# Turned z of the last channel block: one transfer per eight rows, 128-row products, and a new order of the queues

## The chip, the cores and the metric

The kernel runs on one core of a Trainium2 chip. The core has a matrix engine (TensorE, PE in the profile, with its weight loads as PEld), VectorE (DVE), ScalarE (ACT), GpSimd (POOL) and SyncE (SP). SP and POOL are used here mostly to issue transfers: SP feeds queue q1 of the profile's table of queues, POOL feeds q0, and both are served by the same 16 DMA engines. The metric is the device time of one execution in microseconds, the median of several runs; lower is better.

## The reference

An S4 convolution block and an MLP block with adaptive layer normalisation, over one sequence of 2048 positions with 512 channels (D) and 1792 hidden units (F), all in float32. Cut to what matters:

```python
def _A_ref(u, A_re, A_im, B_re, B_im, C_re, C_im, log_dt, Dskip):
    dt = exp(log_dt)[:, None]
    P = exp((dt * (A_re + 1j*A_im))[:, :, None] * arange(L))
    K = einsum("dn,dnl,dn->dl", Cc, P, dt * Bc).real          # a kernel of 2048 taps per channel
    Yf = rfft(pad(u)) * rfft(pad(K))                          # long convolution by FFT
    return irfft(Yf)[:L] + u * Dskip

mod = (silu(c) @ w_mod).reshape(6, D)                         # sa, ca, ga, sb, cb, gb
h = layernorm(x) * (1 + ca) + sa
x = x + ga * _A_ref(h, ...)
h = layernorm(x) * (1 + cb) + sb
x = x + gb * (mish(h @ w1 + b1) @ w2)
```

## The kernel before

**Tiling.** The 512 channels are four blocks of 128 (b = 0 to 3). The Fourier transforms are done as matrix products in two stages, with 64 frequency columns times 32 rows. A block goes through eight steps v = 8b .. 8b+7 (s = v mod 8). In step v, `s_ubu`/`s_ug` and `s_ubk` make the two transforms of the eight rows s, `s_prod` multiplies them on DVE, `s_t1` transposes the result on PE, ACT copies it to the tile `yt`, and `s_invb` (L606) does the first inverse stage on PE (the bank `pib`) with the constants `mi`, copies it on ACT to the tile `z` and writes `z` on SP to DRAM, to `zd[b]`. The tile `z` has three buffers: the copy of step v waits until the write of step v-3 has landed.

**Turning.** The second inverse stage needs the data turned: rows on the partitions. So `zd[b]`, 64 rows of 64 columns times 128 channels, is read back into `zt` tiles. In blocks 0 to 2 that is `s_zl` (L621) and `zt_load` (L615), eight transfers of 64 rows for a whole block once all of its z is written; for the last block it is `zt_rows` (L961) within `drain`, two sets of eight rows at a time in four transfers (one for each group of 16 columns, j, which goes to 32 partitions of its own), and the last two sets singly. `inva_mm` and, for the last block, `inva_half` (L968) are the products of the second inverse stage, into the banks `pia`; `inva_half` contracts 32 partitions into 32 rows for each of 16 places. `inva_add` (L667) adds the residual x on DVE and writes the result to DRAM (`x2d`), on the queue named in `bulk[0]`.

**The drain.** `drain` (L940) is the code between the main loop and the MLP, and where this change mostly sits. Its eight steps v = 24..31 finish the last block, while the weights `w1` are loaded (`w1_load`, POOL, tiles `w1s` with three buffers) and split into high and low parts (`w1_split`, ACT and DVE), and block 2's `zt` is read. Behind the steps come the products of blocks 2 and 3, the bias rows of the MLP (`bias_rows`, `bias_sum`: products of `w1` with a row of the modulation), the layer normalisation of the first quarter of the rows (`ln_stats`, `ln_scales` with `rsqrt`, `ln_qs`), its transposition (`ln_tq`, banks `pln`) and `ln_h`, which makes the left operand `hh` of the MLP. The gate of the MLP, gb, is made early by `gate_row` (L480), written to DRAM as one row and read back to all partitions (`gbb`) in the drain. The last block is called b in `drain`, the third b-1.

**Order.** Instructions of DVE, ACT and PE within the drain are held in the order of the code (`InOrder`), those of DVE and ACT up to the second step f of the MLP; what stands outside this, among it the transfers of SP and POOL, a scheduler orders by priority. Each queue takes its transfers in order: a transfer that waits for a semaphore holds up what stands behind it on that queue.

**The MLP.** Behind the drain, 14 steps f handle the first quarter of the rows with plain products (`mm1_plain`, `mm2`), and `load_w2` (L1049) loads each `w2` piece on SP, multiplies it with `gbb` on DVE, splits it and stores it for the three later quarters.

## Time and profile before

| | us |
|---|---|
| median of 3 runs | 721.03 (718.92 to 723.68) |
| the profiled execution | 722.1 |
| its span, first to last instruction | 720.3 |
| from the drain's first step to the MLP's first product | about 341 to 403 |
| from the MLP's first product to the end | 403.1 to 720.3 |

PE is busy for 641.7 us of the span (89%), DVE for 496.4 (69%), ACT for 373.5 (52%) and POOL for 88.5 (12%). The mean granted PE clock is 0.964 of full speed. The queues moved 116.07 MB, 82.18 MB of it on q1 (SP) and 32.91 MB on q0 (POOL).

Nearly all rows of this profile have line L127, since a helper records every instruction of PE, DVE and ACT; such rows are told apart by their tiles. Transfers have the line of their call. In a timeline a row gives start and length in us, engine, line, operation, out<-in with the shape, the count of instructions merged into it, and in brackets how long the engine had been idle before it and what ended that. A float32 product is recorded as two MATMULs, so that 16 products are x32.

### The profile page before, as it was taken

To read this page: it belongs to the slowest core of one execution; us is meant where nothing else is said; L and a number is where in the kernel's file an instruction comes from. 1 tells how busy PE (TensorE), PEld (TensorE's weight loads), DVE (VectorE), ACT (ScalarE), POOL (GpSimd) and SP (SyncE) were. 2 spreads that over 40 slices of the span, in tenths; PEclk is the share of its full clock that TensorE was granted. 3 is DMA by queue.
4 is the path that set the end of the run, shared out by engine and by line. 5 is a ranking of instruction groups with operands and counts; after the bars stand their busy time and mean duration, and the time that the engine had idled before them with its cause. 6 is when DMAs were issued, how large, how long until landed. Compare 5 with 4: busy or idle time off the path is not lost.

```text
span 720.3 us, 15347 instructions
## 1 busy us (share of the span) xinstructions
PE 641.7 (89%) x6163; PEld 519.9 (72%) x6192; DVE 496.4 (69%) x1008; ACT 373.5 (52%) x620; POOL 88.5 (12%) x178
## 2 busy tenths in 40 slices
PE   0587686999999999999967999989999999999996
PEld 0353354777778877888841788878988898998995
DVE  6999976889899969994843799448336733563332
ACT  3665478556967686664630654443346244443231
POOL 1000530060106200001401000000100010010100
PEclk9969899999999999999978999989999999999999
DMA  9929788674229743565996498627432653264222
GB/s 235 228 110 294 169 193 199 186 178 119 63 72 213 184 118 99 132 180 140 268 216 152 144 325 285 211 71 204 135 117 89 199 163 107 89 190 133 87 88 59
DMA packets 108761, 116.07 MB, mean 161 GB/s; under 512 B 13009, under 2 KB 84945, under 8 KB 108050
## 3 DMA queue, kind: packets, MB, share of 16 engines
q1 hardware_dynamic: 94034, 82.18, 41.7%
q0 software_dynamic: 14656, 32.91, 16.3%
q8 instruction: 49, 0.80, 0.5%
q14 instruction: 22, 0.18, 0.1%
HBM read 80.44 MB, written 32.51 MB: 157 GB/s over the span
## 4 chain that ended last, share of the span: by engine, by line
PE 74%; DVE 10%; DMA 7%; ACT 5%; issue 3%; SPq 1%; DVEq 0%; ACTq 0%
PE pr L127 30%; PE pp L127 10%; PE pub L127 6%; PE pang L127 6%; PE pkb L127 4%; PE pkg L127 4%; PE pib L127 4%; PE pka L127 3%; DVE ec L127 2%; DMA zd<-z 2%; DVE raw L127 2%; PE pt L127 2%; ACT ec L127 2%; PE pbias L127 1%; DMA cT<-in_c 1%
## 5 line engine op out<-in xcount | busy, mean ns | idle before, releaser
L127 DVE TENSOR_TENSOR ec<-ec,m 128x1024 f32<-128x1024 f32 (+1 forms) x96 | 97.4, 1043 | 13.4 <-ACT ec L127 13.1
L127 ACT ACTIVATE ec<-pang 128x1024 f32<-128x1024 f32 x64 | 65.1, 1034 | 53.2 <-PE pang L127 53.2
L127 PE MATMUL pr<-hh,w 128*128 128x256 f32 (+1 forms) x420 | 77.9, 327 | 1.2 <-DVE hh L127 1.2
L127 PEld LDWEIGHTS pr<-hh,w 128*128 128x128 f32 x420 | 67.4, 189 | 12.7 <-DVE hh L127 1.5
L127 DVE TENSOR_TENSOR mh<-x,pr 128x256 f32<-128x256 f32 x63 | 26.4, 420 | 68.4 <-PE pr L127 68.2
L127 PE MATMUL pp<-w,mah 128*128 128x512 f32 x224 | 71.0, 398 | 0.8 <-DVE xf L127 0.8
L127 PE MATMUL pr<-w,mah 128*128 128x512 f32 x224 | 70.4, 396 | 0.0
L127 ACT ACTIVATE mh<-pr,b 128x256 f32<-128x256 f32 (+1 forms) x35 | 19.6, 560 | 80.7 <-PE pr L127 80.7
L127 DVE TENSOR_TENSOR m<-co 128x1024 f32<-128x1024 f32 (+1 forms) x64 | 59.7, 953 | 2.5 <-ACT co L127 2.2
L127 ACT ACTIVATE mh<-mh,b 128x256 f32<-128x256 f32 x63 | 32.1, 510 | 51.4 <-DVE mh L127 51.2
L127 DVE TENSOR_TENSOR mal<-mh,mah 128x512 fp32r<-128x512 f32 x56 | 38.5, 688 | 25.4 <-ACT mah L127 25.4
L1052 POOL DMA_DIRECT2D w<-w2d x42 | 22.2, 529 | 264.5 <-PE pp L127 249.4
L127 PE MATMUL pp<-w,mal 128*128 128x512 f32 x112 | 44.1, 394 | 0.0
L127 PE MATMUL pr<-w,mal 128*128 128x512 f32 x112 | 44.1, 394 | 0.0
L127 PEld LDWEIGHTS pp<-w,mah 128*128 128x128 f32 x224 | 38.5, 190 | 6.0 <-DVE xf L127 1.2
L127 PE MATMUL pka<-bdk,ks 128*64 128x128 f32 x512 | 36.2, 285 | 6.9 <-ACT ks L127 6.9
L339 POOL DMA_DIRECT2D s<-pk x48 | 23.7, 501 | 149.7 <-DVE pk L127 75.6
L127 DVE TENSOR_TENSOR x<-x,pr 128x256 f32<-128x256 f32 x42 | 17.6, 420 | 35.4 <-PE pr L127 35.4
L127 PE MATMUL pib<-yt,mi 128*128 128x128 f32 x256 | 36.5, 288 | 6.2 <-ACT yt L127 6.2
L127 PE MATMUL pr<-hs,wt 128*128 128x256 f32 x252 | 38.2, 288 | 2.8 <-ACT hs L127 2.0
L127 PEld LDWEIGHTS pkg<-ec 128*32 128x32 f32 x2048 | 33.5, 112 | 9.7 <-ACT us L127 4.1
L127 PEld LDWEIGHTS pib<-yt,mi 128*128 128x128 f32 x256 | 32.7, 200 | 10.6 <-ACT yt L127 7.0
(159 smaller groups left out, 1377.4 us busy)
## 6 DMA issues: line engine op xcount, KB each, us to landing
w<-w2d POOLq DMA_DIRECT2D x42, 512.0 KB, 3.6
ud<-us SPq DMA_DIRECT2D x64, 128.0 KB
gu<-ud SPq DMA_DIRECT2D x32, 256.0 KB
zd<-z SPq DMA_DIRECT2D x32, 256.0 KB
w2d<-w SPq DMA_DIRECT2D x14, 512.0 KB
wm<-in_w_mod SPq DMA_DIRECT2D x24, 256.0 KB
zt<-zd SPq DMA_DIRECT2D x16, 256.0 KB
xf<-x2d SPq DMA_DIRECT2D x16, 256.0 KB
```

The lines of the kernel that those rows point to most:

```text
L127: ins = f(*a, **kw)
L339: nc.gpsimd.dma_start(S3[b, i][q, :], pk[32 * i:32 * i + 32, 8 + k, :])
L1052: nc.gpsimd.dma_start(t, w2d[f])
```

## The change

- **zt of the last block.** `zt_rows(s, queue)` reads eight rows of `zd[3]` in one transfer of 256 KB: 32 partitions with 8 KB each, to every fourth partition, beginning with s mod 4. All but the last set go on POOL as soon as their step's z is written; the last (s = 7) goes on SP.
- **mi and di4.** The constants `mi` are permuted, so that the columns of `zd` stand in the order in which the transfers above take 16 at a time, and so that `zt_load` of the other blocks reads 1024 contiguous numbers for each row where it read two pieces of 512. `di4` becomes 128 x 256, for each j with zeros where another j's columns stand.
- **inva_half.** The products of the last block contract all 128 partitions, 16 for each half as before, ordered by j and then by a. `inva_half(0)` stands behind all four `bias_rows` and `gate_row`; of the second half, j = 0 stands first, then the addition and statistics of j = 0, then the rest.
- **Queues.** Block 2's `zt` in the drain moves from POOL to SP. The `x2d` writes of blocks 2 and 3 in the drain move from POOL to SP, behind the last `zt_rows` (`pin["SP"]`), and so do the loads of `w2`.
- **gate_row** is done in the drain: four products of the modulation's column with the identity, and a copy on ACT into `gbb`. The early product, the DRAM row, and the 256 KB read are gone.
- **DVE.** The multiplications of `w2` with `gbb` that were free of the order (f = 2 and later) now come behind the last ordered DVE instruction. The first normalisation writes to a new tile `xn` instead of in place, and `rsqrt` there saves one instruction. The additions of j = 1 to 3 stand ahead of `ln_tq`, and the four `bias_rows` in a row.

```diff
+        dj[:, j, :, :, j, :] = da.T.reshape(2, 4, 8, 32).transpose(2, 1, 0, 3) / 2048.0
...
     def gate_row():
         p = bank("pgb")
-        T.matmul(p, mean.to_broadcast([P, P]), MRW[4], start=True, stop=True)
-        t = cv.tile([P, D], F32, tag="q2", name="gbr", bufs=1)
-        A.copy(t, p)
-        nc.sync.dma_start(gbd, t[0:1])
+        for b in range(NB):
+            T.matmul(p[:, b * P:b * P + P], modp[:, 4, b:b + 1].to_broadcast([P, P]), ident, start=True, stop=True)
+        A.copy(MW["gbb"], p)
...
             bulk[0].dma_start(ZT[b, j4, a][64 * h + r0:64 * h + r1],
-                              view(zd[b], (64 * r0 + 4 * (j4 + h) + 16 * a) * P,
-                                   [[64 * P, r1 - r0], [16 * P, 2], [1, 512]]))
+                              view(zd[b], (64 * r0 + 16 * (j4 + h) + 4 * a) * P, [[64 * P, r1 - r0], [1, 1024]]))
...
-        bulk[0].dma_start(x2d[b][:, 4 * j:4 * j + 4, :], x)
+        after(bulk[0].dma_start(x2d[b][:, 4 * j:4 * j + 4, :], x), pin.get("SP"))
...
-        nc.gpsimd.dma_start(MW["gbb"], view(gbd, 0, [[0, P], [1, D]]))
-        def zt_rows(s0, s1):
-            h, r0, r1 = s0 // 4, 8 * (s0 % 4), 8 * ((s1 - 1) % 4 + 1)
-            for j in range(4):
-                nc.sync.dma_start(zt[32 * j + r0:32 * j + r1, h],
-                                  view(zd[b], ((32 * h + r0) * 64 + 4 * j) * P,
-                                       [[64 * P, r1 - r0], [16 * P, 4], [1, 512]]))
+        def zt_rows(s, queue):
+            return queue.dma_start(zt[s % 4::4, s // 4], view(zd[b], 8 * s * 64 * P, [[16 * P, 32], [1, 2048]]))
...
-            for a in range(4):
-                for j in range(4):
-                    r = slice(32 * j, 32 * j + 32)
-                    T.matmul(PIA[b, j][32 * a:32 * a + 32, :], di4[r, 32 * h:32 * h + 32], zt[r, h, a, :],
+            for j in js:
+                for a in range(4):
+                    T.matmul(PIA[b, j][32 * a:32 * a + 32, :], di4[:, h, j, :], zt[:, h, a, :],
                              start=(h == 0), stop=(h == 1), skip_group_check=True)
...
             if i in (1, 2):
-                on_pool(s_zl, v0 - 6 + 2 * i)
-            if i in (2, 4, 6):
-                zt_rows(i - 2, i)
-        zt_rows(6, 7)
-        zt_rows(7, 8)
-        bulk[0] = nc.gpsimd
+                s_zl(v0 - 6 + 2 * i)
+            if i >= 2:
+                zt_rows(i - 2, nc.gpsimd)
+        zt_rows(6, nc.gpsimd)
+        pin["SP"] = zt_rows(7, nc.sync).ins
...
-        bias_rows(0)
-        bias_rows(1)
-        inva_half(0)
-        inva_half(1)
+        for n in range(4):
+            bias_rows(n)
+        gate_row()
+        p = psum.tile([P, 2, 512], F32, tag="pa", name="pia2", bufs=1)
+        PIA.update({(b, 0): bank("pia"), (b, 1): bank("pia"), (b, 2): p[:, 0], (b, 3): p[:, 1]})
+        inva_half(0, range(4))
+        inva_half(1, (0,))
         inva_add(b, 0)
         ln_stats(0, (b,))
-        bias_rows(2)
-        bias_rows(3)
+        inva_half(1, range(1, 4))
         ln_scales(0)
         bias_sum()
-        ln_qs(0)
+        xn = cv.tile([P, 4, NB, P], F32, tag="gk", name="xn", bufs=1)
+        ln_qs(0, xn)
+        for j in range(1, 4):
+            inva_add(b, j)
...
-        nc.sync.dma_start(raw, view(io["B_w2"], f * P * D, [[D, P], [1, D]]))
-        V.tensor_mul(raw, raw, MW["gbb"])
+        after(nc.sync.dma_start(raw, view(io["B_w2"], f * P * D, [[D, P], [1, D]])), pin["SP"])
+        after(V.tensor_mul(raw, raw, MW["gbb"]), pin.get("V"))
```

What the scheduler makes of it, at three places. On SP, from the first z of the last block (`z24`; `zd3` is that block's z in DRAM, `zt3` its turned tile, `zt2..` are block 2's), before:

```order
L613 DMA zd3_139<-z25_4486 128x4x128
L964 DMA zt3_4408<-zd3_139 16x4x512
L613 DMA zd3_139<-z26_4532 128x4x128
L964 DMA zt3_4408<-zd3_139 16x4x512 x3
L613 DMA zd3_139<-z27_4580 128x4x128
L613 DMA zd3_139<-z28_4618 128x4x128
L613 DMA zd3_139<-z29_4658 128x4x128
L1055 DMA w2s0_4977<-in_B_w2 128x512
L964 DMA zt3_4408<-zd3_139 16x4x512 x4
L613 DMA zd3_139<-z30_4686 128x4x128
L964 DMA zt3_4408<-zd3_139 16x4x512 x4
L613 DMA zd3_139<-z31_4713 128x4x128
```

and after:

```order
L625 DMA zd3_138<-z24_4439 128x4x128
L629 DMA zt202_4485<-zd2_137 64x1024 x2
L625 DMA zd3_138<-z25_4479 128x4x128
L564 DMA gu31_4518<-ud_139 128x4x128
L629 DMA zt220_4528<-zd2_137 64x1024
L625 DMA zd3_138<-z26_4525 128x4x128
L629 DMA zt220_4528<-zd2_137 64x1024
L629 DMA zt222_4531<-zd2_137 64x1024 x2
L625 DMA zd3_138<-z27_4570 128x4x128
L625 DMA zd3_138<-z28_4609 128x4x128
L625 DMA zd3_138<-z29_4646 128x4x128
L625 DMA zd3_138<-z30_4675 128x4x128
```

No read of `zt3` stands between the z writes any more; block 2's reads stand among the first four instead. On POOL, over the same steps (`w1s` are the loads of the MLP's weights), before:

```order
L617 DMA zt200_4489<-zd2_138 64x2x512
L808 DMA w1s3_4417<-in_B_w1 128x896
L617 DMA zt200_4489<-zd2_138 64x2x512
L617 DMA zt202_4492<-zd2_138 64x2x512
L808 DMA w1s4_4457<-in_B_w1 128x896
L617 DMA zt202_4492<-zd2_138 64x2x512
L808 DMA w1s5_4503<-in_B_w1 128x896
L617 DMA zt220_4535<-zd2_138 64x2x512 x2
L617 DMA zt222_4538<-zd2_138 64x2x512 x2
L808 DMA w1s6_4553<-in_B_w1 128x896
L808 DMA w1s7_4591<-in_B_w1 128x896
```

and after:

```order
L817 DMA w1s3_4410<-in_B_w1 128x896
L817 DMA w1s4_4450<-in_B_w1 128x896
L970 DMA zt3_4401<-zd3_138 32x2048
L817 DMA w1s5_4496<-in_B_w1 128x896
L970 DMA zt3_4401<-zd3_138 32x2048
L817 DMA w1s6_4543<-in_B_w1 128x896
L970 DMA zt3_4401<-zd3_138 32x2048
L817 DMA w1s7_4582<-in_B_w1 128x896
L970 DMA zt3_4401<-zd3_138 32x2048 x4
```

Each `w1s` from the sixth on now stands behind a read of `zt3`, which waits for a z write of SP. On DVE, from the addition of j = 0 on (`w2s` times `gbb` is a piece of the MLP's second weights), before:

```order
L127 TENSOR_TENSOR xt_3085<-xt_3085,pia 128x512
L127 TENSOR_TENSOR w2s_5027<-w2s_5027,gbb 128x512
L127 BN_STATS bst_4724<-xt_3085 128x6 x4
L127 BN_AGGR mv_365<-bst_4724 128x2 x4
L127 TENSOR_SCALAR rsq_4854<-mv_365 128x4
```

and after:

```order
L131 TENSOR_TENSOR xt_3079<-xt_3079,pia 128x512
L131 BN_STATS bst_4705<-xt_3079 128x6 x4
L131 BN_AGGR mv_364<-bst_4705 128x2 x4
L131 TENSOR_SCALAR rsq_4841<-mv_364 128x4
L131 TENSOR_SCALAR rst_365<-rsq_4841 128x4
```

The multiplication left its place between the addition and the statistics.

More of the change, by code (lines that the diff above doesn't have):

```diff
@@ L70, in _constants @@
     da = da.transpose(0, 2, 1).reshape(32, 64)
+    dj = np.zeros((8, 4, 4, 2, 4, 32))
+    for j in range(4):
+        dj[:, j, :, :, j, :] = da.T.reshape(2, 4, 8, 32).transpose(2, 1, 0, 3) / 2048.0
     ac = np.zeros((4, 32, 32, 32))
@@ L95, in _constants @@
         "mf": np.ascontiguousarray(mf.transpose(1, 0, 2).reshape(P, 32 * P)).astype(f),
-        "mi": np.ascontiguousarray(mf.transpose(2, 0, 1).reshape(P, 32 * P)).astype(f),
+        "mi": np.ascontiguousarray(mf.transpose(2, 0, 1).reshape(P, 32, 2, 4, 4, 4).transpose(0, 1, 2, 4, 3, 5)
+                                   .reshape(P, 32 * P)).astype(f),
         "bdk": np.ascontiguousarray(bdk.transpose(0, 1, 2, 4, 3)).reshape(P, 256).astype(f),
@@ L99, in _constants @@
         "di": np.tile(da.T / 2048.0, (2, 1)).astype(f),
-        "di4": np.tile(da.T.reshape(2, 32, 32).transpose(1, 0, 2).reshape(32, 64) / 2048.0, (4, 1)).astype(f),
+        "di4": dj.reshape(P, 256).astype(f),
         "ac": ac.reshape(P, 1024).astype(f),
@@ L148, in s4_block, with after @@
     gen = right.enter_context(tc.tile_pool(name="gen", bufs=2, side="right"))
-    last = [None]
+    last, pin = [None], {}
+    def after(ins, first):
+        if first is not None:
+            tc.add_manual_dep(ins.ins, first.name,
+                              mybir.DependencyInfo(mybir.DependencyClass.NoSync, mybir.DependencyReason.DATA),
+                              reason="order of issue")
+        return ins
     def chain(ins):
@@ L218, in s4_block @@
     di = cst.tile([P, 32], F32, name="di")
-    di4 = cst.tile([P, 64], F32, name="di4")
+    di4 = cst.tile([P, 2, 4, 32], F32, name="di4")
     mf = cst.tile([P, 32, P], F32, name="mf")
@@ L476, in mod_out @@
         V.tensor_scalar(modp[:, s, :], PM[s][:, :NB], float(s in (2, 3)), None, op0=OP.add)
-    gbd = dram.tile([1, D], F32, name="gbd")
     def gate_row():
         p = bank("pgb")
-        T.matmul(p, mean.to_broadcast([P, P]), MRW[4], start=True, stop=True)
-        t = cv.tile([P, D], F32, tag="q2", name="gbr", bufs=1)
-        A.copy(t, p)
-        nc.sync.dma_start(gbd, t[0:1])
+        for b in range(NB):
+            T.matmul(p[:, b * P:b * P + P], modp[:, 4, b:b + 1].to_broadcast([P, P]), ident, start=True, stop=True)
+        A.copy(MW["gbb"], p)
     sab = cst.tile([P, D], BF16, name="sab")
@@ L508, in shift_rows, with rsqrt @@
         A.copy(sab, a)
-    def rsqrt(dst, var, n, pool, tag):
+    def rsqrt(dst, var, n, pool, tag, half=True):
         t = pool.tile([P, n], F32, tag=tag, name=tag)
@@ L514, in rsqrt @@
         V.tensor_scalar(dst.bitcast(I32), t.bitcast(I32), -0.5, 1597463007.0, op0=OP.mult, op1=OP.add)
-        V.tensor_scalar(t, t, -0.5, None, op0=OP.mult)
+        if half:
+            V.tensor_scalar(t, t, -0.5, None, op0=OP.mult)
         for _ in range(3):
             V.tensor_mul(t2, dst, t)
-            V.tensor_mul(t2, t2, dst)
+            if half:
+                V.tensor_mul(t2, t2, dst)
+            else:
+                V.scalar_tensor_tensor(t2, t2, -0.5, dst, op0=OP.mult, op1=OP.mult)
             V.scalar_tensor_tensor(dst, t2, 1.5, dst, op0=OP.add, op1=OP.mult)
@@ L752, in s4_block @@
     at(0, norm_scales)
-    at(20, lambda: nc.sync.dma_start(di4, io["di4"]))
+    at(20, lambda: nc.sync.dma_start(di4.rearrange("p h j i -> p (h j i)"), io["di4"]))
     at(5, lambda: nc.sync.dma_start(mi.rearrange("p a b -> p (a b)"), io["mi"]))
@@ L761, in s4_block @@
         at(n + 3, mod_out, i)
-        if i == 4:
-            at(n + 2, gate_row)
     at(MR, shift_ratio)
@@ L866, in ln_scales, with ln_q, ln_qs @@
             V.bn_aggr(mv2[:, 4 * tt + q, :], LST[tt][:, q].rearrange("p b s -> p (b s)"))
-        rsqrt(rst2[:, 4 * tt:4 * tt + 4], mv2[:, 4 * tt:4 * tt + 4, 1], 4, keep, "rsq2")
+        rsqrt(rst2[:, 4 * tt:4 * tt + 4], mv2[:, 4 * tt:4 * tt + 4, 1], 4, keep, "rsq2", False)
     PL = {}
-    def ln_q(tt, q):
+    def ln_q(tt, q, dst=None):
         i = 4 * tt + q
         x = LNX[tt][:, :, q, :]
-        V.tensor_scalar(x, x, mv2[:, i, 0:1], rst2[:, i:i + 1], op0=OP.subtract, op1=OP.mult)
+        V.tensor_scalar(x if dst is None else dst, x, mv2[:, i, 0:1], rst2[:, i:i + 1], op0=OP.subtract, op1=OP.mult)
     nm2 = keep.tile([P, 4], F32, name="nm2")
-    def ln_qs(tt):
+    def ln_qs(tt, XN):
         V.scalar_tensor_tensor(nm2, mv2[:, 4 * tt:4 * tt + 4, 0], -1.0, rst2[:, 4 * tt:4 * tt + 4], op0=OP.mult,
@@ L882, in ln_qs, with ln_tq @@
             if q % 2:
-                x = LNX[tt][:, :, q, :]
-                A.activation(x, x, AF.Identity, scale=rst2[:, 4 * tt + q:4 * tt + q + 1], bias=nm2[:, q:q + 1])
-            else:
-                ln_q(tt, q)
-    def ln_tq(tt, q, b):
+                A.activation(XN[:, q], LNX[tt][:, :, q, :], AF.Identity, scale=rst2[:, 4 * tt + q:4 * tt + q + 1],
+                             bias=nm2[:, q:q + 1])
+            else:
+                ln_q(tt, q, XN[:, q])
+    def ln_tq(XN, q, b):
         if q == 0:
             PL[b] = bank("pln")
-        T.transpose(PL[b][:, P * q:P * q + P], LNX[tt][:, b, q, :], ident)
+        T.transpose(PL[b][:, P * q:P * q + P], XN[:, q, b, :], ident)
     def ln_norm(tt):
@@ L956, in drain, with inva_half @@
         s_xp(v0 - 1)
-        nc.gpsimd.dma_start(MW["gbb"], view(gbd, 0, [[0, P], [1, D]]))
         bulk[0] = nc.sync
         zt = big.tile([P, 2, 4, 512], F32, tag="gk", name="zt3")
-        def zt_rows(s0, s1):
-            h, r0, r1 = s0 // 4, 8 * (s0 % 4), 8 * ((s1 - 1) % 4 + 1)
-            for j in range(4):
-                nc.sync.dma_start(zt[32 * j + r0:32 * j + r1, h],
-                                  view(zd[b], ((32 * h + r0) * 64 + 4 * j) * P,
-                                       [[64 * P, r1 - r0], [16 * P, 4], [1, 512]]))
-        def inva_half(h):
-            if h == 0:
-                p = psum.tile([P, 2, 512], F32, tag="pa", name="pia2", bufs=1)
-                PIA.update({(b, 0): bank("pia"), (b, 1): bank("pia"), (b, 2): p[:, 0], (b, 3): p[:, 1]})
-            for a in range(4):
-                for j in range(4):
-                    r = slice(32 * j, 32 * j + 32)
-                    T.matmul(PIA[b, j][32 * a:32 * a + 32, :], di4[r, 32 * h:32 * h + 32], zt[r, h, a, :],
+        def zt_rows(s, queue):
+            return queue.dma_start(zt[s % 4::4, s // 4], view(zd[b], 8 * s * 64 * P, [[16 * P, 32], [1, 2048]]))
+        def inva_half(h, js):
+            for j in js:
+                for a in range(4):
+                    T.matmul(PIA[b, j][32 * a:32 * a + 32, :], di4[:, h, j, :], zt[:, h, a, :],
                              start=(h == 0), stop=(h == 1), skip_group_check=True)
@@ L1014, in drain @@
             inva_add(b - 1, j)
-        bias_rows(0)
-        bias_rows(1)
-        inva_half(0)
-        inva_half(1)
+        for n in range(4):
[5 more added lines that the diff above has]
+        inva_half(1, (0,))
         inva_add(b, 0)
         ln_stats(0, (b,))
-        bias_rows(2)
-        bias_rows(3)
+        inva_half(1, range(1, 4))
         ln_scales(0)
         bias_sum()
-        ln_qs(0)
+        xn = cv.tile([P, 4, NB, P], F32, tag="gk", name="xn", bufs=1)
+        ln_qs(0, xn)
+        for j in range(1, 4):
+            inva_add(b, j)
         for q in range(4):
             for c in range(NB):
-                ln_tq(0, q, c)
+                ln_tq(xn, q, c)
         for c in range(NB):
@@ L1031, in drain @@
         bias_add()
-        for j in range(1, 4):
-            inva_add(b, j)
-        bulk[0] = nc.sync
     drain()
@@ L1211, in s4_block @@
         if f == 2:
+            pin["V"] = ordered["V"]
             del ordered["V"], ordered["A"]
```

## The prediction

> **What bounds the kernel now.** I read the page's slices first, then the chain of work that ended last between 330 and 420 us, then the timeline and the stretches at the places that the chain names. Every time below is in us from the span's start. The page's slices of 18 us each:

> ```profile
> PE   0587686999999999999967999989999999999996
> ...
> DMA  9929788674229743565996498627432653264222
> ```

> Behind the start, PE is full except in the 21st and 22nd slice (6 and 7, from 360 to 396), which is the drain. From the MLP's first product on, PE has 307.2 busy us of 317.19 (last row below), so nothing but PE's own work counts there, and the change leaves that work as it is.

> ```profile
> 340.00:345.00 5.00, 4.18 (x33) 3.64 (x32) 4.23 (x8) 2.23 (x4) 2.17 (x5) 1.00 0.87 219
> ...
> 364.80:369.40 4.60, 0.00 (x0) 0.00 (x0) 0.46 (x1) 1.91 (x3) 0.00 (x0) 0.86 0.92 243
> 369.40:376.00 6.60, 5.11 (x20) 4.28 (x20) 5.30 (x14) 2.01 (x3) 0.00 (x0) 0.50 1.03 200
> ...
> 403.11:720.30 317.19, 307.20 (x1770) 268.87 (x1770) 169.01 (x384) 128.91 (x240) 23.83 (x45) 0.99 0.49 153
> ```

> The columns are stretch, length, busy time of PE, PEld, DVE, ACT and POOL, PE clock, DMA share, GB/s. The chain through the drain (start, length, what):

> ```profile
> 356.29 11.12 DMA zd<-z
> ...
> 376.16 0.59 ACT z L127
> ...
> 376.78 4.56 DMA zd<-z
> ...
> 381.35 0.65 SPq L964
> ...
> 382.05 6.55 DMA zt<-zd
> ...
> 388.64 3.39 PE pia L127 x30
> 392.03 8.03 PE pbias L127 x60
> ...
> 402.30 0.76 DVE hh L127
> ...
> 403.11 10.03 PE pr L127 x42
> ```

> So three things set when the MLP's first product (`pr`) starts: a z write of 11.12 us, the round trip of the last z through DRAM, and the products and the normalisation behind it. The copies of z on ACT show what the long write does:

> ```profile
> 343.94 0.59 ACT L127 COPY z<-pib 128x512 f32<-128x512 f32 x1 [0.66 <-PE pib L127]
> ...
> 351.66 0.59 ACT L127 COPY z<-pib 128x512 f32<-128x512 f32 x1 [0.15 <-PE pib L127]
> ...
> 359.37 0.59 ACT L127 COPY z<-pib 128x512 f32<-128x512 f32 x1 [0.15 <-PE pib L127]
> ...
> 367.49 0.59 ACT L127 COPY z<-pib 128x512 f32<-128x512 f32 x1 [4.64 <-DMA zd<-z]
> ```

> Five copies (v = 24 to 28) stand 3.86 apart ((359.37 - 343.94) / 4). The sixth needs the buffer of v = 26 and comes 8.12 behind the fifth; PE then has nothing for 4.60 and works at clock 0.50 afterwards. The write of v = 26 was late for two reasons. It was issued late, at 356.29, though its copy ended at 352.25: SP stood at a read of `zt3` that waits for the write before. And it was slow:

> ```profile
> q0 software_dynamic: 475, 1.95, 92.6%
> q1 hardware_dynamic: 419, 0.27, 12.3%
> ```

> These rows are the queues between 354 and 362 (packets, MB, share): POOL's queue took nearly all, with packets of 4.1 KB in the mean (1.95 MB by 475), while SP's, of 0.64 KB (0.27 by 419), got 0.27 MB in 8 us.

> **The change, part by part.**

> *A, the z writes.* No read of `zt3` is left between them on SP, so v = 26 is issued when its copy ends, 4 us earlier. Block 2's reads (eight of 256 KB) leave POOL for SP, where they stand ahead of the writes of v = 24 to 27. Does the write of v = 27 land before v = 30 wants its buffer? At 3.86 a step, v = 30 is copied at 359.37 + 2 x 3.86 = 367.1.

> ```profile
> DMA packets 3869, 5.99 MB, mean 266 GB/s; under 512 B 333, under 2 KB 2840, under 8 KB 3867
> ...
> w1s<-in_B_w POOLq DMA_DIRECT2D x4, 448.0 KB, 8.3
> zt<-zd POOLq DMA_DIRECT2D x6, 256.0 KB, 7.7
> zd<-z SPq DMA_DIRECT2D x4, 256.0 KB
> ```

> From 345 to 367.5 the chip moved 5.99 MB, and 1.10 from 340 to 345 (219 GB/s above): 7.1 MB in 27.5 us, 258 GB/s with the engines full. With the change, from 340 until v = 27 is written, there are 8 reads of block 2 (2.10 MB), 4 z writes (1.05), 2 reads `gu` of the same 256 KB (0.52), 5 loads `w1s` (2.29) and three of the new `zt3` reads (0.79), 6.75 MB in all: 26.2 us, to 366.2. By bytes the wait goes, with 0.9 to spare; the 256 KB of `gbb` and the early `w2` are not among them any more. The order within the queues can still cost: SP's writes stand behind block 2's reads, and POOL's bursts win against SP's short packets as above. The last `w1s` stands on POOL behind the `zt3` read that waits for v = 26: if that lands near 358, 8.3 later is 366, just ahead of the ACT cast that wants it behind the copy of v = 30. The eight reads cost SP an issue each (0.65 by the chain's SP row), 5.2 spread over 15 us in which SP has little else. Bounds for what is left of the wait: 0 and the 4.64 of the row. I take 1.0, near the byte sum. Then the last z copy begins at 359.37 + 3 x 3.86 + 1.0 = 371.95 instead of 376.16: **4.2 gained**.

> *B, from there to the end of the product j = 0.* Before, 376.13 (the end of PE's `pib`) to 392.03, 15.9 us, with the 6.55 of `zt3`'s read in it. Rows for the prices, the first from block 0 at full clock:

> ```profile
> 232.45 1.09 PE L127 MATMUL pia<-zt,di 64*32 64x512 f32 x16
> ...
> 364.12 0.63 PE L127 MATMUL pt<-ident,ug 128*128 128x128 f32 x4 [0.26 <-DVE ug L127]
> ...
> 376.06 3.03 PE L127 MATMUL pia<-zt,di 64*32 64x512 f32 x32
> 379.02 3.21 PE L127 MATMUL pbias<-w,modp 128*32 128x512 f32 x32
> 382.16 1.16 PE L127 MATMUL pia<-zt,di 32*32 32x512 f32 x32
> ...
> 396.78 3.29 PE L127 MATMUL pbias<-mean,br 128*128 128x1 f32 x28
> 399.93 1.94 PE L127 MATMUL pln<-ident,xt 128*128 128x128 f32 x16
> ```

> After, PE has in order: block 2's products, 2 x 1.09 = 2.1 (the 3.03 came right behind the stretch at clock 0.50); four bias rows, 2 x 3.21 = 6.4; the gate's four, 0.6 by the transposes `pt` of that shape; the first half of the last block and then j = 0 of the second. These products contract 128 rows into 32 columns, the form of `pbias`, of which four stand beside each other: 3.21 us for 2 x 512 + 2 x 384 = 1792 columns is 1.79 ns a column, 0.92 for four products of 512. The first half is four of those, 3.7, and j = 0 one, 0.9. Lower bound: the old form, 1.16 for sixteen; upper: the same at half clock, 7.4 and 1.8. I take the `pbias` price, the same form. Sum 13.7, so j = 0 ends at 371.95 + 13.7 = 385.65, against 392.03: **another 2.2**. The transfer hides behind this: its copy ends at 372.5, and with the old price of write, issue and read (4.56 + 0.65 + 6.55) it would be there at 384.3, while j = 0 starts at 384.7. One read of 256 KB should be quicker than the four before. Without that cover each us of it would count. The gate's copy and the bias copies on ACT lie beside PE's products.

> *C, from j = 0 to the first `pr`.* Before, 392.03 to 403.11, 11.1.

> ```profile
> 392.12 0.69 DVE L127 TENSOR_TENSOR xt<-xt,pia 128x512 f32<-128x512 f32 x1 [10.64 <-PE pia L127]
> 392.73 0.69 DVE L127 TENSOR_TENSOR w2s<-w2s,gbb 128x512 f32<-128x512 f32 x1
> 393.33 0.87 DVE L127 BATCH_NORM_STATS2 bst<-xt 128x6 f32<-128x128 f32 x4
> ...
> 395.16 0.17 DVE L127 TENSOR_SCALAR rsq<-rsq 128x4 f32<-128x4 f32 x1
> 395.37 0.16 DVE L127 TENSOR_TENSOR rsq<-rst,rsq 128x4 f32<-128x4 f32 x1
> ...
> 397.22 1.00 DVE L127 TENSOR_SCALAR xt<-xt,mv,rst 128x512 f32<-128x512 f32 x2
> 397.34 1.52 ACT L127 ACTIVATE xt<-xt,nm,rst 128x512 f32<-128x512 f32 x2
> ...
> 405.01 1.88 DVE L127 TENSOR_TENSOR xp<-xp,pia 128x512 f32<-128x512 f32 x3
> ```

> The vector chain ran from 392.03 to 398.86 (end of the ACT row), 6.8; it loses the `w2s` multiplication (0.6 from start to start) and one `rsqrt` instruction (0.2): 6.0. PE meanwhile does the other three j (2.75) and the 28 small `pbias` (3.29), also 6.0; before, it had bias rows there and let `pln` start only at 399.93. From `pln` to `pr` it was 3.2. So 9.2: **1.9 gained**. The three additions (1.88) move ahead of `hh` on DVE. The last normalising row on DVE ended at 398.22, 6.2 behind j = 0; 0.8 less and 1.88 more is 7.3. `hh` wants DVE at about 6.0 + 2.4 (399.93 to 402.30, the chain's DVE row) = 8.4. If that cover goes, they cost what passes 1.1.

> *D, edits costed at nothing.* The `w2` loads now stand behind the last `zt3` read and four `x2d` writes on SP, so they go out near 380; they are wanted behind the first mish of the MLP, near 399, and there lies their cover. The moved multiplication adds 0.7 to DVE in the MLP, where the additions (1.88) went away. The permuted constants, `di4`, the early gate and block 0 and 1's longer rows lie in a stretch where PE is full. The later `rsqrt` saving is off the path.

> Sum: 4.2 + 2.2 + 1.9 = 8.3. The profiled execution, 722.1 (span 720.3 and 1.8 around it), becomes 713.8. It stood 1.1 above the median of 721.03, so the median becomes **712.7**.

> **The rivals.**

> *The wait stays (R1).* Block 2's bytes are only put on another queue, and SP's writes now stand behind them in one ring. If what limits the sixth copy is the shared engines, A gives nothing: 721.03 - 4.1 = 716.9. For it: 1.03 of 1.00 DMA share in the stretch from 369.4; `w1s` and `zt3` bursts remain on POOL. Against it: 12.3% for q1 beside 92.6%, and 4 us of the late write were SP's own wait. [...]

> *Half clock (R2).* After the 4.60 us gap PE worked at 0.50 for the whole next 6.6 us. If the last steps leave gaps like that again, about 6.8 us of B's dense products run at half clock and cost half of it, 3.4: 716.1. Against it: without the wait no gap of that length is left; the earlier steps of the drain kept 1.00. [...]

> *Slower (R3).* The z writes starve. At 0.27 MB in 8 us (34 GB/s) a 256 KB write takes 7.7 us, against 3.86 a step; with v = 29, 30 and 31 each late by 3.86, the last copy begins at 382.5, and B and C bring `pr` at 405.4, 2.3 behind before: 723.3, and 728 and more if four or five writes suffer. It decides once the last `pib` ends behind 403.11 - 9.2 - 13.7 = 380.2. Against it: POOL has 448 + 256 KB a step to move for three steps, 187 GB/s of 258, and only 68 behind the last `w1s`.

> *More (R4).* No wait at all and a shorter step for v = 30 and 31, which have no transform of u: 710 and below.

> **How the numbers follow.** Forecast 0.50, R1 0.20, R2 0.15, R3 0.05, R4 0.10. A measurement of this kernel tells about 1% from no change, 7.2 us: faster means below 713.8. The forecast's own range is 710 to 716 (wait 0 to 3.6, products between the bounds), of which some 0.8 lies below 713.8; with R4 and a little of R1 and R2 that is 0.55 for faster, 0.40 for the same, 0.05 for slower. The range takes R4 and R1 and R2 together: 708 to 719.

> **What would show it.** A: the z copies 3.9 apart to the end and the last near 372; wrong if a copy waits for `zd<-z` by more than 2. The clock from 365 to 396 should be 1.00. B: `pia` of 128*32 at about 0.9 for eight records, no PE idle time ahead of j = 0; wrong if PE waits for `zt<-zd`. C: 9.2 from the end of j = 0 to `pr`, with no `w2s` among it. D: 317 from `pr` to the end; if PE waits there for `w` or `wt`, the loads moved on SP were wanted earlier than I think.

## The result, and the profile after

| | before | changed |
|---|---|---|
| median of 12 runs, us | 723.75 (718.92 to 727.08) | 716.08 (708.36 to 720.59) |
| ratio, changed to before | | 0.9885 (95%: 0.9848 to 0.9923) |
| profiled execution, us | 722.1 | 715.37 |
| its span, us | 720.3 | 713.6 |

The medians differ by 7.7 us (1.06%). Two runs of the changed kernel, 720.55 and 720.59, count as slow; they are in its median but not in the ratio, which gives 1.15%. The interval of the ratio lies below 1, so the gain is clear of the noise, though small. The three runs shown before the prediction are among the twelve of the left column, whose median is 2.7 above theirs (721.03). The page's slices of the changed kernel:

```profile
PE   0587687999999999999979999989999999999996
...
DMA  9929798674239643565984797536433652364322
```

Of the two holes in the drain the second is gone (the 22nd slice, 7 before, is 9). The first is a 7 where it was a 6. Four stretches show where the time went. Each is read from rows of ACT or DVE, so that the same events bound it in every kernel: A from ACT's first copy of `yt` behind 340 (step v = 24) to its last copy of `z` (v = 31); B from there to DVE's addition of the last block's j = 0 to `xt`; C from there to ACT's first `hh`; D from there to the end.

| us | A | B | C | D | span |
|---|---|---|---|---|---|
| before | 34.05 | 15.96 | 9.46 | 318.7 | 720.3 |
| changed, first profile | 32.13 | 14.36 | 7.24 | 318.2 | 713.6 |
| changed, second profile | 29.12 | 13.57 | 7.64 | 317.4 | 711.0 |

The second profile is a run of the same kernel, told of below. Of the kernel before there is this one profile, so each gain read from the table carries the spread of single executions. The kernels start A between 340.1 and 343.3, which is the rest of the span.

The timeline of ACT in the changed kernel's first profile, copies of `z` of v = 24, 28, 29 and 31 and the cast of the `w1` part 6:

```profile
343.47 0.59 ACT L131 COPY z<-pib 128x512 f32<-128x512 f32 x1 [0.66 <-PE pib L131]
...
358.89 0.59 ACT L131 COPY z<-pib 128x512 f32<-128x512 f32 x1 [0.15 <-PE pib L131]
...
362.73 0.59 ACT L131 COPY z<-pib 128x512 f32<-128x512 f32 x1 [0.36 <-PE pib L131]
365.57 0.94 ACT L131 CAST w<-w1s 128x896 fp32r<-128x896 f32 x1 [2.26 <-DMA w1s<-in_B_w]
...
373.76 0.58 ACT L131 COPY z<-pib 128x512 f32<-128x512 f32 x1 [2.17 <-PE pib L131]
```

The copy of v = 29, which had waited 4.64 for a z write, waits for no transfer. Three us later ACT waits 2.26 for a load of `w1`, and everything behind ACT waits with it. The queues between 354 and 362 (packets, MB, share), the stretch in which SP's queue had moved 0.27 MB before:

```profile
q0 software_dynamic: 202, 1.16, 52.5%
q1 hardware_dynamic: 759, 0.99, 51.9%
```

SP's queue moved 0.99 MB; block 2's own reads, now on this queue, are among them, so the figure is no measure of the z writes alone. What the late load did to PE, from PE's timeline:

```profile
367.05 1.16 PE L131 MATMUL pib<-yt,mi 128*128 128x128 f32 x8 [2.11 <-ACT yt L131]
369.83 1.09 PE L131 MATMUL pt<-ident,ug 128*128 128x128 f32 x4 [1.63 <-DVE ug L131]
371.65 2.08 PE L131 MATMUL pib<-yt,mi 128*128 128x128 f32 x8 [0.73 <-ACT yt L131]
373.66 2.73 PE L131 MATMUL pia<-zt,di 64*32 64x512 f32 x32
376.32 6.22 PE L131 MATMUL pbias<-w,modp 128*32 128x512 f32 x64
382.47 1.16 PE L131 MATMUL pgb<-ident,modp 128*128 128x128 f32 x8
383.55 7.07 PE L131 MATMUL pia<-zt,di 128*32 128x512 f32 x64
390.56 3.29 PE L131 MATMUL pbias<-mean,br 128*128 128x1 f32 x28
393.71 1.94 PE L131 MATMUL pln<-ident,xn 128*128 128x128 f32 x16
```

Two gaps of 2.11 and 1.63, and the `pib` behind them takes 2.08 where the one before takes 1.16: half clock. From 371.65 to `pln` PE then has no gap, and never waits for `zt`. The stretches that show the clock (length, busy time of PE, PEld, DVE, ACT, POOL, PE clock, DMA share, GB/s):

```profile
365.07:368.48 3.41, 1.16 (x8) 0.97 (x8) 1.94 (x3) 1.66 (x3) 0.53 (x1) 1.00 0.57 197
368.48:375.31 6.83, 4.75 (x28) 2.94 (x36) 3.82 (x12) 2.36 (x4) 1.56 (x3) 0.50 0.67 193
375.31:378.72 3.41, 3.41 (x51) 0.95 (x39) 3.04 (x8) 0.41 (x1) 0.00 (x0) 1.00 0.47 127
...
396.88:713.60 316.72, 307.00 (x1769) 268.66 (x1769) 167.45 (x379) 128.89 (x240) 22.17 (x42) 0.99 0.49 152
```

### The profile page after: what moved, and what is told of

The parts are those of the page before. It is cut to its first block, busy times and chain, and to the rows that moved or that the text cites. A ratio compares the mean times of both kernels' runs of the same rounds, so it can differ in the third digit from the quotient of the medians.

```text
span 713.6 us, 15368 instructions
## 1 busy us (share of the span) xinstructions
PE 644.3 (90%) x6198; PEld 521.5 (73%) x6198; DVE 495.8 (69%) x1004; ACT 373.2 (52%) x620; POOL 82.5 (12%) x168
## 4 chain that ended last, share of the span: by engine, by line
PE 76%; DVE 9%; DMA 6%; ACT 5%; issue 3%; SPq 1%; POOL 0%; ACTq 0%; DVEq 0%; POOLq 0%
PE pr L131 31%; PE pp L131 11%; PE pang L131 7%; PE pub L131 6%; PE pkb L131 4%; PE pkg L131 4%; PE pib L131 4%; PE pka L131 3%; DVE ec L131 2%; DVE raw L131 2%; PE pia L131 2%; PE pt L131 2%; ACT ec L131 2%; DMA w1s<-in_B_w 1%; PE pbias L131 1%
## 5 line engine op out<-in xcount | busy, mean ns | idle before, releaser
L131 ACT ACTIVATE mh<-mh,b 128x256 f32<-128x256 f32 x63 | 32.1, 510 | 50.5 <-DVE mh L131 50.3
L131 PE MATMUL pang<-rnd,oneb 128*128 128x512 bf16 x128 | 42.7, 416 | 0.0
L350 POOL DMA_DIRECT2D s<-pk x48 | 25.2, 564 | 148.5 <-DVE pk L131 75.7
L131 PE MATMUL pang<-ac,s 128*128 128x256 f32 x128 | 30.5, 322 | 11.4 <-ACT ec L131 11.3
## 6 DMA issues: line engine op xcount, KB each, us to landing
gu<-ud SPq DMA_DIRECT2D x32, 256.0 KB, 3.4
zd<-z SPq DMA_DIRECT2D x32, 256.0 KB, 3.6
zt<-zd SPq DMA_DIRECT2D x25, 256.0 KB, 5.4
wm<-in_w_mod SPq DMA_DIRECT2D x24, 256.0 KB, 3.8
xf<-x2d SPq DMA_DIRECT2D x16, 256.0 KB, 5.6
```

The lines of the kernel that those rows point to most:

```text
L131: ins = f(*a, **kw)
L350: nc.gpsimd.dma_start(S3[b, i][q, :], pk[32 * i:32 * i + 32, 8 + k, :])
```

## The experiments

The theory after this first profile: no copy waits for a z write any more, and what is left of A's wait is a load of `w1` that arrives late; behind it the clock falls. The rivals are that bytes in flight, not queues, set the wait, and that PE's own rows do. The runs are single executions with a profile, apart from two, e9 and e12, that were timed in six. All stretches in us:

| run | what differs from the changed kernel | A | B | C | D | span |
|---|---|---|---|---|---|---|
| e1_reads_gpsimd | block 2's reads back on POOL | 32.27 | 14.68 | 9.56 | 320.1 | 717.2 |
| e2_reads_behind | nothing, in effect | 30.71 | 14.99 | 9.27 | 320.8 | 717.3 |
| e3_no_w1 | three `w1` loads left out | 28.19 | 13.58 | 7.34 | 317.8 | 709.2 |
| e4_bias_early | half the bias rows, gate into the steps | 30.44 | 9.35 | 8.44 | 317.4 | 706.6 |
| e5_reads_late | four of block 2's reads held back | 28.19 | 19.03 | 7.80 | 317.4 | 713.4 |
| e6_early_mixed | e4, means among other products | 30.15 | 9.35 | 7.69 | 317.0 | 704.3 |
| e7_zt_on_sync | last block's reads on SP | 29.55 | 14.09 | 7.23 | 318.3 | 709.8 |
| e8_early_mixed_late | e6 and e5 | 29.51 | 10.26 | 7.69 | 317.1 | 705.1 |
| e9_mixed_on_sync | e6 and e7 | 29.52 | 9.34 | 7.69 | 317.3 | 706.9 |
| e10_changed_again | nothing | 29.12 | 13.57 | 7.64 | 317.4 | 711.0 |
| e11_free_multiply | `pin["V"]` gone | 29.22 | 13.58 | 9.18 | 320.8 | 714.5 |
| e12_zt_on_sync_timed | as e7 | 28.92 | 14.45 | 7.24 | 318.4 | 709.6 |

**Block 2's reads back on POOL.**

```diff
-                s_zl(v0 - 6 + 2 * i)
+                on_pool(s_zl, v0 - 6 + 2 * i)
```

> Block 2's four last reads of z are issued by GpSimd again, as before the change; everything else stays changed. Theory Q (which queue holds the reads decides how fast the z writes go): a scalar copy of z waits for a z write again, by 3 us or more, and the last one ends at 376 us or later (376.2 before, 373.8 changed). Rival B (only the bytes in flight count, not the queue): no wait on a z write beyond 0.5 us, last copy at 373.8 +- 0.7.

ACT's copy of v = 29 and the queues between 354 and 362 in this run:

```profile
364.17 0.59 ACT L131 COPY z<-pib 128x512 f32<-128x512 f32 x1 [2.86 <-DMA zd<-z]
```

```profile
q0 software_dynamic: 480, 2.03, 90.8%
q1 hardware_dynamic: 401, 0.20, 11.4%
```

The wait for a z write is back (2.86, a shade under the 3 that was named), with the shares of the kernel before. In the trace all eight reads went to POOL, not only the last four that the expectation names. The write that was waited for, that of v = 26, from the chain of this run (start, length):

```profile
350.73 13.36 DMA zd<-z
```

It was issued right behind its copy, with no standing of SP ahead of it, and took 13.36; in the four profiles of the changed kernel (the first, e2, e10 and e11) the same write took 8.0, 7.6, 5.9 and 6.5. So which queue holds the reads did decide here how fast this write went. The sum hardly differs, 2.23 MB on the two queues here and 2.15 in the changed kernel in the same 8 us; what changed is which transfers landed first. But neither theory's end time came: the last copy is at 372.85, not 376, because A began 1.05 earlier and no `w1` load was late here. A is 32.27, as in the first profile of the changed kernel, and 3.1 more than in the second; what the wait costs in time is therefore not shown by this run.

**The last block's reads behind the `w1` loads.** `zt_rows(0)`, `(1)` and `(2)` were written into step i = 4.

```diff
-            if i >= 2:
+            if i == 4:
+                zt_rows(0, nc.gpsimd)
+                zt_rows(1, nc.gpsimd)
+            if i >= 4:
                 zt_rows(i - 2, nc.gpsimd)
```

> The first three reads of the last block's z are issued only in step i = 4, behind the last load of a w1 half, so no load of a w1 half stands behind a read that waits for z writes. Theory O (the load came late because the GpSimd queue stood at a read): the scalar casts wait for no load, the last z copy is at 371 to 372.5 us (373.8 in the changed kernel). Rival B (the load came late because the transfers share their bytes): a load or a z write is as late as before and the last copy stays at 373.8 +- 0.7.

The edit did nothing: transfers are placed by the scheduler, and in the trace POOL issues reads and loads in the changed kernel's order (reads at 349.97 and 354.34, loads at 351.69 and 354.87). So theory O was not tested, though the copy at 372.28 falls into its band. The run counts as another profile of the changed kernel.

**Three `w1` loads less.** For n >= 5 `w1_load` takes the tile of part n - 3 and loads nothing.

```diff
     def w1_load(n):
+        if n >= 5:
+            WS[n] = WS[n - 3]
+            return
```

> The loads of w1 parts 5, 6 and 7 are left out; parts 2, 3 and 4 are cast a second time in their place, so the output is not the reference's. Theory W (the load that came late took what the missing z wait gave): last z copy at 371 to 372, the cast of part 6 waits for nothing, and the clock in the stretch 367 to 376 stays near 1.00 because TensorE has no gap. Rival P (TensorE or VectorE is what the last four steps wait for, the load only ends the same time): last copy stays within 0.7 of 373.8.

A is 28.19, no cast waits, and the clock is 1.00 from 362 to 391: theory W. So 28.2 is what DVE, ACT and PE need for the eight steps; the first profile had 3.9 above it, waiting and the half clock behind it.

**Bias rows and gate in the last steps.**

```diff
+            if i == 7:
+                bias_rows(1)
             s_t1(v)
+            if i == 6:
+                bias_rows(0)
+            if i == 7:
+                gate_row()
...
-        for n in range(4):
+        for n in range(2, 4):
             bias_rows(n)
-        gate_row()
```

> Bias rows 0 and 1 and the gate row are made inside the last two steps, where TensorE had gaps of 2.1 and 1.6 us; only bias rows 2 and 3 stand between block 2's products and the last block's. Theory P (from the last z copy on TensorE's own instructions set the time): the drain from the first of yt's copies to the first product of the MLP is 3.5 to 4.5 us shorter than the changed kernel's 55.25 us. Rival L (the last read of z sets the time, TensorE's rows only fill it): less than 1 us shorter, and TensorE waits for zt.

From the first `yt` to the second `pr` it is 49.76, 5.5 less than 55.25, more than the 4.5 named. B is 9.35, and 4.23 less than the 13.58 of e3, which has the same full clock there. What the moved products cost in the steps, from this run's chain:

```profile
364.55 1.85 PE pbias L131 x16
...
367.49 1.43 PE pbias L131 x16
...
369.51 0.89 PE pgb L131 x8
```

Together that is 4.17. So PE's own instructions set B, and `zt` is not waited for: theory P. Of the 5.5, 3.8 lie behind the last `z`; the other 1.7 are A's, where the load was late by 0.83 and 0.15 instead of 0.58 and 2.26 and the clock stayed at 1.00.

**Four reads of block 2 held back.** They are tied behind a z write.

```diff
-            if i in (1, 2):
-                s_zl(v0 - 6 + 2 * i)
+            if i in (1, 5):
+                pin["zl"] = pin["z"] if i == 5 else None; s_zl(v0 - 4 if i == 1 else v0 - 2)
...
```

(`pin["z"]` is the last z write; `zt_load` issues its transfers `after` `pin["zl"]`. In step i = 5 the last z write is that of v = 29, not that of v = 28 as the expectation has it: in the trace v = 28 was written at 358.88, v = 29 at 362.51, and the held reads go out from 362.92.)

> Four of block 2's eight reads of z (1 MB) are held back until the z write of v = 28 has been issued; nothing else differs from the changed kernel. Theory W (1 MB too much in flight before 366 makes the w1 load late): no scalar cast waits for a load by more than 0.3 us, from the first copy of yt to the last copy of z 28.2 to 29 us (32.1 in the changed kernel), clock 1.00 from 366 to 376. Rival (the order on GpSimd's queue alone makes it late): the cast of part 6 still waits by 2 us and the distance stays at 31.5 or more. A third way: the held reads come late for block 2's products, and TensorE waits for zt behind the last pib.

Theory W holds for A: 28.19, to 0.01 the time with three loads left out, and no cast waits. So 1 MB less in flight before 366 frees the load, and the queue order is not needed to explain it. But the third way came too. PE's timeline:

```profile
369.09 2.07 PE L131 MATMUL pia<-zt,di 64*32 64x512 f32 x24
372.41 1.04 PE L131 MATMUL pia<-zt,di 64*32 64x512 f32 x2 [1.25 <-DMA zt<-zd]
373.80 1.55 PE L131 MATMUL pia<-zt,di 64*32 64x512 f32 x6 [0.34 <-DMA zt<-zd]
```

The held reads came too late for block 2's products, PE waited 1.25 and 0.34 us, the clock fell to 0.50 (374.22 to 377.64), and B became 19.03. The 3.9 gained in A are lost in B. Held behind v = 28, as was meant, they could have started about 3.6 us earlier; whether that would have been in time was not tried.

**The means among other products.** On top of e4, `bias_sum(fs)` is called in three parts.

```diff
-    def bias_sum():
+    def bias_sum(fs):
...
-        inva_half(1, range(1, 4))
+        for j in range(1, 4):
+            inva_half(1, (j,))
+            bias_sum(range(5 * j - 5, min(5 * j, FB)))
         ln_scales(0)
-        bias_sum()
```

> The kernel with the early bias rows, and in it the 14 one-column products of the bias means are put in fives behind each of the last three products j = 1, 2, 3, instead of in one row behind them. Theory T (the row of one-column products looks idle to the clock and halves it): clock 1.00 from the end of j = 0 to the first pr and beyond, the 16 transposes pln 1.60 to 1.95 us instead of 2.70, and the first pr 1 us nearer to the last z copy (19.3 before). Rival (the clock falls by its own count of time, whatever the mixture): clock 0.5 for 3 us or more between pln and pr, no gain.

The stretches of e4 around the means, and the whole drain of this run:

```profile
383.17:386.58 3.41, 3.41 (x34) 3.37 (x31) 3.07 (x14) 1.27 (x2) 0.00 (x0) 1.00 0.31 111
386.58:390.00 3.42, 3.28 (x17) 2.88 (x15) 1.46 (x4) 1.03 (x3) 0.00 (x0) 0.50 0.57 186
```

```profile
362.00:388.82 26.82, 25.36 (x238) 13.04 (x237) 17.26 (x52) 9.89 (x16) 2.09 (x4) 1.00 0.66 204
```

Behind the row of one-column products e4 ran 3.42 us at half clock, although PE shows no idle time ahead of it. With the same products mixed the clock stays at 1.00; C is 0.75 shorter. This one execution cannot carry theory T, since the changed kernel's first profile kept 1.00 there without any mixing; the last section has more on it.

**The last block's reads on SP, profiled and timed.**

```diff
-                zt_rows(i - 2, nc.gpsimd)
-        zt_rows(6, nc.gpsimd)
+                zt_rows(i - 2, nc.sync)
+        zt_rows(6, nc.sync)
```

> The seven early reads of the last block's z go back to SyncE, between its z writes, still as one transfer of eight rows each. Theory S (SyncE standing at a read delayed the z writes before the change): z writes are again issued 3 us or more behind their copies, a scalar copy of z waits for a write by 3 us or more and the last z copy comes 34 us or more behind the first copy of yt (32.1 changed, 34.05 before). Rival N (four transfers a read and 8-row strides were the cost, not the place): no wait on a write, 32 us or less; with GpSimd's queue free of waiting reads the w1 loads come early and it may even be 30.

> The changed kernel with the last block's reads of z on SyncE, timed. If the one look holds (52.40 us from the first yt to the first pr against 55.25): ratio to the kernel before 0.980 to 0.986. If the look was a lucky one: the changed kernel's own 0.9885 within 0.003.

No z write is late: in e7 SP issues two of them at 354.43 and 358.52, right behind copies that ended at 354.41 and 358.49. So what theory S forecast did not come. But its condition hardly came either. SP's waits at reads of `zt3` (us in total, times, the longest), before, from 345 to 385, and in e7, from 338 to 378:

```profile
SPq L964 <- DMA zd<-z: 8.3, 3, 6.9
```

```profile
SPq L970 <- DMA zd<-z: 2.8, 2, 2.1
```

A read that has one set, singly, and stands two writes behind the one that it waits for finds its data there, or nearly; the longer wait of e7 ended at 364.68, and the next z write went out at 365.81, as its copy ended. The run shows that reads on SP do no harm when they are placed so; that a standing SP would do none is not shown. The only cast that waits, in e7, does so by 0.35. A is 29.55 and 28.92. The time does not follow: 716.21 (6 runs, 711.40 to 719.97) against 723.36, ratio 0.9890 (0.9844 to 0.9937), the changed kernel's own. So the move of these reads to POOL, as against this order on SP, neither gained nor cost anything that can be measured.

**All three.**

> The early bias rows, the mixed mean products and the held-back reads of block 2 together. If the three gains are apart: from the first yt to the last z copy 28.5 to 29.5 us, from there to the first pr 18.3, MLP 316, span about 704. If the bias rows in the last steps fill the gaps that the late load makes, then without the gaps they only move: first to last as 30.4 with the bias rows alone, span 706.

From the first `yt` to the last `z` 29.51, but block 2's products take 2.79 for 1.88, and the span is 705.1: the gains do not add. With the gaps filled by bias rows the late load costs little (A is 30.15 in e6, where the reads are not held, 0.64 more than here), and the held reads cost 0.9.

**The changed kernel again.**

> The changed kernel once more, as a control for the single looks. If the late w1 load is a property of the kernel: the cast of part 6 waits for it by 1.5 to 3 us, 31.5 us or more from the first yt to the last z copy (32.13 in the first profile), and the clock halves between 366 and 376. If it came by chance: no cast waits by more than 1 us, 30.5 or less.

Between the two answers. ACT's cast and the two stretches before the last `z`:

```profile
362.15 0.94 ACT L131 CAST w<-w1s 128x896 fp32r<-128x896 f32 x1 [1.05 <-DMA w1s<-in_B_w]
```

```profile
365.30:368.71 3.41, 1.94 (x16) 1.54 (x14) 3.12 (x6) 1.63 (x3) 0.18 (x1) 1.00 0.90 298
368.71:372.12 3.41, 1.80 (x14) 1.40 (x13) 2.62 (x8) 2.01 (x3) 1.39 (x3) 1.00 0.69 193
...
392.60:396.02 3.42, 3.28 (x11) 2.29 (x10) 2.25 (x4) 2.42 (x4) 0.00 (x0) 0.50 0.87 249
```

A load is late in this profile too, that of part 5, by 1.05, and the clock does not fall in the steps. A is 29.12. Together with e2 and e11, which have the same order there, A is 32.13, 30.71, 29.12 and 29.22: some load of `w1` is late in each (part 5, part 6 or both, by 0.5 to 2.3), so the lateness is a property of the kernel; its size and the clock's answer differ from one execution to the next.

**The multiplication not held back.**

```diff
-            pin["V"] = ordered["V"]
```

> The multiplication of w2 by the gate is no longer held behind the last instructions of the drain on VectorE; it goes back ahead of the addition of j = 0, as before the change. Theory C (the vector chain from j = 0 sets when the transposes pln start): the first xn on ScalarE comes 0.5 to 0.7 us later behind j = 0 and the first pr too, if TensorE has nothing else to do by then. Rival P (TensorE's own rows, three products and the means, end at the same time): pr moves by less than 0.3.

VectorE ahead of j = 0:

```profile
383.37 0.69 DVE L131 TENSOR_TENSOR w2s<-w2s,gbb 128x512 f32<-128x512 f32 x1 [7.99 <-DMA w2s<-in_B_w]
384.51 0.69 DVE L131 TENSOR_TENSOR xt<-xt,pia 128x512 f32<-128x512 f32 x1 [0.44 <-PE pia L131]
```

The multiplication comes while DVE waits for j = 0, and ACT's first `xn` is 4.53 behind the addition (384.51 to 389.04), as in e10 (385.94 to 390.47). Neither theory: in this profile the pin costs and saves nothing. C and D are longer here for another reason, the clock behind the means:

```profile
386.09:389.50 3.41, 3.41 (x35) 2.57 (x26) 3.00 (x19) 0.46 (x1) 0.00 (x0) 1.00 0.23 80
389.50:399.74 10.24, 10.10 (x35) 8.24 (x35) 5.01 (x9) 3.48 (x6) 0.00 (x0) 0.50 0.76 222
```

**The version that beats both.** Early bias rows, mixed means, and the last block's reads on SP.

> The early bias rows, the mixed mean products and the last block's reads of z on SyncE together. If the load's wait and TensorE's rows are separate: first yt to last z copy 29 to 29.6 us (30.15 without the reads on SyncE), from there to the first pr 18.5, clock 1.00 throughout, profiled span 703 to 704, ratio to the kernel before about 0.974. If the early bias rows already cover the load's wait, nothing is added: 30.1 and the span 704.3 +- 0.7.

```profile
363.00:391.16 28.16, 27.16 (x255) 14.68 (x253) 18.58 (x54) 11.06 (x18) 0.00 (x0) 1.00 0.72 229
```

PE is busy 27.16 of 28.16 us at full clock. Timed: 709.15 (6 runs, 707.63 to 710.28) against 723.36, ratio 0.9794 (0.9751 to 0.9837). That is 14.2 us below the kernel before, and the interval lies below the changed kernel's, if narrowly (0.9837 against 0.9848). The expected 0.974 was too much; what the reads on SP add to e6, which was not timed, is not to be seen.

## Why the prediction came out as it did

The forecast was a gain of 8.3; 7.7 were measured, and the two profiles of the changed kernel give 6.7 and 9.3 by span. The median stands 3.4 above the 712.7 that was named, but 2.7 of that is the kernel before, whose median rose with more runs; it is just outside the forecast's own 710 to 716 and within 708 to 719. The 1.15% lies just beyond the 1% at which the chances divided faster (0.55) from the same (0.40). All three terms are there; that their sum came so near is in part luck, since the terms missed in both directions from one execution to the next, and D, put at nothing, gave some.

*A (4.2).* The mechanism holds: no copy waits for the z buffer, because the write of v = 26 is issued 4.5 us earlier (351.79 for 356.29) and is less crowded out (8.0 us, against 13.36 in e1, where the wait is back). The gain was 1.9 in the first profile and 4.9 in the second. The step that failed is the one on what is left of the wait: it put 1.0 on a z write and found the last `w1` load "just ahead of the ACT cast that wants it". It was the load before that, part 6, that came late. From POOL's timeline of the changed kernel's first profile:

```profile
354.44 0.51 POOL L970 DMA_DIRECT2D zt<-zd  x1 [2.11 <-DMA zd<-z]
354.97 0.56 POOL L817 DMA_DIRECT2D w1s<-in_B_w  x1
360.33 0.51 POOL L970 DMA_DIRECT2D zt<-zd  x1 [4.80 <-DMA zd<-z]
...
367.76 0.53 POOL L970 DMA_DIRECT2D zt<-zd  x1 [6.34 <-DMA zd<-z]
```

Part 6 went out at 354.97, behind a read that waited for a z write until 353.89, and was 10.58 under way where 8.3 had been the median. The byte sum itself came out: it had the write of v = 27 landed by 366.2, and the read of the last row, which waits for that write, goes out at 367.76; the write had landed at 367.48, 12.05 behind its issue. So the z writes are not all quick. At the pace of e3 (7.3 from the copy of v = 28 to that of v = 30) its buffer would have been wanted at 366.2, and the 1.0 taken for this wait would not have been far off; the later load hides it. But the sum was drawn for the z writes alone, and ACT wants loads from the same bytes sooner. So the core of the rival R1, that the shared engines limit the steps, is half right: e5 shows that 1 MB held back removes the wait altogether. The prediction asked only whether the old wait stays, not who waits instead.

*R2, and "the clock from 365 to 396 should be 1.00".* This failed. R2 was tied to R1's gap of 4.60, on the ground that without it no gap of that length is left. Gaps of 2.11 and 1.63 were enough: 6.83 us at 0.50. It cost 1.4 of A in the first profile (`pib` 2.08 for 1.16, `pt` 1.09 for 0.63) and 0.8 of B (block 2's products 2.73 for the 1.95 of the second profile), where the second lost nothing.

*B (13.7 from `pib` to the end of j = 0; 2.2 gained).* Right at full clock: 13.57 by the stretch in e10, 14.36 with the fall. The prices held: 6.22 for the bias rows (6.4 taken), 0.88 for four products over 128 partitions (0.92 taken). The gate was priced at 0.6 and took 1.1, since a product of that kind is recorded twice (`pgb`, four products, x8) and the transposes that gave the price are not (`pt`, four of them, x4, 0.63). That PE sets B, and the transfer hides, is shown by e4: 4.17 of PE's rows taken out shorten B by 4.23.

*C (9.2; 1.9 gained).* 8.8 from j = 0 to the same `pr`. The vector chain from the addition to the first `xn` on DVE is 4.41 (388.12 to 392.53), against 5.10 before (392.12 to 397.22): the multiplication did leave it. That `pin["V"]` is needed for it was not said, and in e11 it isn't.

*D (0).* 0.5 and 1.3. PE waits for none of the loads moved to SP in the MLP. Where D is longer (320.1 to 320.8 in e1, e2, e11) the half clock behind the means reaches into it.

*R3 and R4.* The slow z writes that R3 feared came in part (8.0, 12.05 and 9.0 for v = 26 to 28 in the first profile, against the 7.7 that it named), but each has three steps until its buffer is wanted, and no copy waited. R4's 710 lies inside the spread of the changed kernel (708.36 at best) and is the rule only in e9.

What share of the spread between runs is the clock? Each run has its mean granted clock on record. Of the twelve runs of the changed kernel the fastest (708.36) had 0.980 and the two slowest (720.55 and 720.59) had 0.959 and 0.962; a straight line through the twelve gives 5.3 us for each 0.01, and leaves a scatter of 1.3 us where there were 3.4. So most of the spread goes with the clock. Eleven later runs of the kernel before (median 723.36) have 0.962 in the middle, the changed kernel 0.969: an estimate from these two numbers and such a line through each set (4.4 and 5.3 us for 0.01) is that 3 to 4 of the 7.7 us go with the clock as well. How much of that the shorter gaps in the drain earned stays open, since these means cover the whole span.

## What to carry to other kernels

When a wait is taken away from a stretch whose DMA engines are full, work out the landing time of every transfer that the stretch wants, not only of the one that was late: here the wait of 4.64 for a z write went, and in the first profile ACT waited 2.26 for a load instead, which was 10.58 under way where 8.3 had been the median. A hole in PE can be closed by work that is due anyway: in e4 loads were still late, by 0.83 and 0.15, but A and B together took 39.79 us, against 46.49 and 42.69 in the first and the second profile, and the clock was 1.00 from 363 to 386.58. That, with the mixed means and the reads on SP beside it, brought about as much again (14.2 us in all, where the change alone had 7.7). And do not size a step by one profile: two executions of the same order differed by 3.0 us in one stretch.

## What the hardware showed that was not expected

```profile
368.28:375.12 6.84, 6.04 (x44) 3.16 (x44) 3.51 (x11) 1.44 (x3) 1.03 (x2) 0.50 0.61 192
375.12:392.18 17.06, 17.06 (x166) 7.39 (x159) 6.95 (x30) 3.08 (x6) 0.00 (x0) 1.00 0.42 140
392.18:402.42 10.24, 10.10 (x35) 8.31 (x35) 5.11 (x10) 3.58 (x6) 0.00 (x0) 0.50 0.75 223
```

6.84, 17.06 and 10.24 are two, five and three times 3.41. The windows below are steps of 3.41 us, laid from the edges that a profile shows. In the one ahead of a fall PE was busy for anything from 0.08 us to all of it:

- In the drain, the clock fell behind windows in which PE was busy for 0.08, 1.01 (both before), 1.16 (the changed kernel's first profile), 1.40 (e7), 1.49 (e2), 1.56 (e1), 1.56 (e12) and 1.82 us (e5) of 3.41, and stayed up behind 1.58 (before, 381.73 to 385.14), 1.77 (e11), 1.78 (e5), 1.80 and 1.94 (e10), 1.88 and 2.11 (e3). The two sets overlap, 1.58 kept and 1.82 lost, so in these profiles no busy time parts them.
- It also fell behind windows in which PE is shown as busy for all of the 3.41 us, with the row of 28 records of one-column products in them (3.29 us at full clock). In seven profiles the part of the row in the window ahead of the fall was 2.15 (e1), 2.47 (e2), 2.18 (e3), 3.29 (e4), 2.66 (e5), 2.48 (e10) and 2.56 us (e11), by the row's start and end. In the four others an edge of the grid cut the row so that no window had more than 1.82 (the changed kernel's first profile), 1.73 (e7), 1.91 (e12) and 2.02 (before), and the clock stayed. Mixed with other products they had no fall in three profiles (e6, e8, e9); but no stretch at 0.50 there places a grid, and by where one would lie the fullest window of e6 held anything from 1.57 to 2.49 us of them. So that mixing keeps the clock up is not shown.

That either of these is what sets the clock is read off the profiles, not tried by an experiment of its own.
